# A first chunk in two halves, output stores ahead in SyncE's queue, and half of the attention output transposed by DMA

## The chip, the cores and the metric

The kernel runs on 1 core of one Trainium2 chip. The metric is the device time of one execution in microseconds (us); five runs of the kernel before gave 276.07 to 276.96, median 276.46. The engines are named as in the profile: PE (TensorE matmul) with PEld (its weight loads), DVE (VectorE), ACT (ScalarE), POOL (GpSimd) and SP (SyncE). POOL and SP issue the DMAs; POOL's are those that convert float32 to float16 on the way.

## What is computed

Attention with two kinds of heads, and then a gated feed-forward layer over its output (the reference, cut):

```python
B, H, S, D = 4, 8, 768, 64          # is_retrieval = [1,0,1,0,0,0,1,0]
scores = q @ k.T / sqrt(D)
# heads 0, 2, 6: causal mask; the others: causal, and key < 4 or query - key < 64
a = softmax(where(mask, scores, -1e9));  x = (a @ v)  # tokens x 512, 3072 tokens
g = x @ w_gate;  val = x @ w_val                      # 512 -> 1536 each
ffn = (gelu(g) * val) @ w_out                         # 1536 -> 512
out = x + sigmoid(x @ w_res) * ffn
```

## The kernel before, in words

**Chunks.** The 3072 tokens are six chunks of 512 tokens (four tiles of 128), `CHUNKS` in line 25. A chunk goes through attention, then gate and value, then output. Attention works on four pairs of heads in the order (0,2), (1,3), (4,6), (5,7). For each pair PE computes scores (L783, and L871 for the four sink keys), ACT takes the exponentials (L799, L878), DVE multiplies by masks (L835), PE weighs the values (L900, L910, L924), and DVE divides by the sums (L950 the reciprocals, L961 a float16 copy `x16`, L963 the float32 copy `xtok`; in the even pairs from the second chunk on, the float16 copy is a cast on ACT or DVE, L969/L970). When two pairs are done, four tiles by two column blocks of `x16` are transposed on PE into PSUM (L978, `to_features`, four 128x128 transposes a block) and copied to `xT` by ACT or DVE (L985).

**Gate and value** (`gate_value`, L1003). For each of 12 blocks of 128 hidden columns (f = 0 to 11), PE multiplies `xT` (four column blocks of 128 by 512 tokens) with `wg` and `wv`: 4 + 4 matmuls of 512 columns, those of the column blocks 0 and 1 first and those of 2 and 3 as a second task. ACT takes gelu (L1015), DVE the product (L1017). **Output** (`output`): `res` (L1031), tanh (L1034), 12 matmuls with `wo` a tile (`ff`, L1046), two DVE steps (L1050, L1053), and the store, issued by SP (L1056).

**Loads.** POOL issues, in this order at the start: q and k of the first chunk in four DMAs, four value tiles, `wg` and `wv` in three column parts each (part j serves f = 4j to 4j+3), q and k of the second chunk, `wr`, `wo` in four parts, then value tiles of the second and third chunk. For the first two chunks q and k are transposed on PE (L646); from the third chunk on they are transposed by SP's DMAs (L684, `dT`, 128x512 each, 128 KB in float16). A copy of the values that is shifted by 64 keys (`vs`) is made by two DVE copies in the first chunk (L594) and by SP's DMAs later (L608).

**The order of the work.** A planner in the kernel (`Graph.schedule`) places every task on its engine's queue when the program is built. It holds a price for each task, takes among the ready tasks the one with the lowest priority number, and for a DMA adds an issue time, a transfer time, 0.8 and 1.6 us, and an extra `late` (L289 to L294). `HINTS` (L42) overrides the priorities of single tasks by their number. An engine then works its queue strictly in that order: a task whose input is late holds all tasks behind it. Two rules stand at the end of `build_kernel`: a chunk's scores come after the gate and value of f = 10 of the chunk before (L1090), and its exponentials after that chunk's last gelu (L1092). PE's idle time at the start is filled with matmuls on zeros (L1062, "warm"), which end with the task `g0`.

**PSUM.** Eight banks are shared by kinds (L479): the first chunk's weighted values use `av0`, three slots of two banks; gate and value use `gv`.

Of the kernel before, what the change touches and what calls it, by code (L numbers as in the profile page):

```python
# [6 lines left out]
DHEAD = 64  # L7
# [29 lines left out]
ROWS_UNTIL = 2  # L37

# [4 lines left out]
    "3:-21.19 5:-58.49 6:-58.34 403:490.65 425:595.32 427:528.41 578:-99.99 586:59.9 611:1499.22 612:516.59 "  # L43
    "622:576.96 635:549.35 636:510.21 637:1538.66 643:580.14 647:570.57 648:558.53 649:1085.71 650:1520.19 "
    "653:525.88 654:576.91 655:1026.63 659:511.56 665:514.73 666:516.61 668:1537.73 671:15.77 673:62.65 "
    "677:0.03 679:80.17 680:-75.91 683:82.91 684:-86.3 685:102.37 686:529.24 689:511.01 701:88.3 702:-1.38 "
    "703:114.98 707:516.6 719:1104.93 722:2562.67 733:1538.65 734:1503.99 756:501.37 777:2386.85 816:2334.5 "
    "855:2510.01 861:1434.93 874:2134.02 886:2457.99 922:3352.32 923:1980.91 924:1487.38 972:2502.01 "
    "996:3513.25 1004:2538.32 1026:1534.33 1040:3534.81 1067:2441.52 1090:4509.27 1095:4498.99 1113:4499.01 "
    "1136:4429.99 1139:3502.04 1181:4467.35 1251:4123.82 1253:4130.53 1262:4510.02 1322:5341.74 1368:4505.02 "  # L50
    "1370:5425.02 1394:5537.53 1399:5528.12 1411:5499.01 1412:4524.63 1418:5505.02 1423:5573.53 1424:5090.24 "
    "1444:5424.01 1446:4529.17 1457:5122.53 1458:6525.69 1468:5116.43 1482:4952.05 1485:6442.5 1510:5505.99 "
    "1553:5511.01 1554:5505.99 1608:7485.06 1628:7447.37 1653:7483.11 "
# [391 lines left out]
def build_kernel(nc, q, k, v, w_gate, w_val, w_out, w_res, out):  # L445
# [34 lines left out]
        "av1": (2, one(0, 1)), "av2": (1, [(0, 1)]), "av0": (3, [(0, 1), (6, 7), (2, 3)]),  # L480
        "sc": (2, [(2, 3), (4, 5)]), "scr": (3, one(5, 4, 3, 2)), "scr0": (3, one(6, 5, 4, 3, 2)),
        "gv": (4, one(6, 7, 5, 4, 3, 2)), "gv0": (4, one(6, 7, 5, 4)), "gv00": (2, one(6, 7)), "out": (2, one(6, 7)), "warm": (1, one(7, 5, 1)),
# [56 lines left out]
    def load_weights():  # L539
        for j in range(3):  # L540
            for nm, t, src in (("g", wg, w_gate), ("v", wv, w_val)):
                s = slice(j * 512, (j + 1) * 512)
                wtok[nm, j] = dma("pool", -20 + j, 2.6, (lambda t=t, s=s: lambda: t[:, :, s])(),
                                  src[:, s].rearrange("(ci p) f -> p ci f", p=128))
        wtok["r"] = dma("pool", -12, 2.6, lambda: wr[:, :, :], w_res.rearrange("(ci p) f -> p ci f", p=128))
        for j in range(4):
            s = slice(j * 3, (j + 1) * 3)
            wtok["o", j] = dma("pool", -11 + j, 1.95, (lambda s=s: lambda: wo[:, s, :])(),
                               w_out[j * 384:(j + 1) * 384, :].rearrange("(fi p) c -> p fi c", p=128))

# [14 lines left out]
    def values(b, a, z, base, each, on_engines=False):  # L565
# [21 lines left out]
        if on_engines:  # L587
            ts = []
            for dst, src, off in ((0, 64, 1), (64, 0, 0)):
                def vs(on, dst=dst, src=src, off=off):  # L590
                    def fn(e):
                        o = at(BB.vs)[dst:dst + 64, a_ - 1:z - 1, :, :].rearrange("p i h d -> p (i h d)")
                        i_ = at(BB.v)[src:src + 64, a_ - off:z - off, :, :].rearrange("p i h d -> p (i h d)")
                        return e.activation(out=o, in_=i_, func=AF.Copy) if on == "act" else e.tensor_copy(out=o, in_=i_)  # L594
                    return fn
                n_ = (z - a_) * 520
                ts.append(G.flex({"dve": (c_dve(n_, 3.0, False), vs("dve")), "act": (c_act(n_), vs("act"))},
                                 [BB.vtok[i - off] for i in range(a_, z)], 130, bufs=[BB.v, BB.vs], name="vs"))
            for i in range(a_, z):
                BB.vstok[i] = ts  # L600
            late_copies.extend(ts)
            return
# [13 lines left out]
    def loads_rows(c, si, b, a, z):  # L616
# [18 lines left out]
        values(b, a, z, base + (10 if c == 0 else 8), False, c == 0)  # L635

        per = 1 if c == 0 or n == 4 else 2
        for k_ in range(0, NPAIR, per):
            ps_ = ORDER[k_:k_ + per]
            pr = 1000 * c - 492 + ps_[0] if c else 40 * k_ - 5  # L640
# [29 lines left out]
    def loads_natural(c, si, b, a, z):  # L670
# [5 lines left out]
        for i in range(a, z):  # L676
            for j, src in ((1, k), (0, q)):
# [6 lines left out]
                t = G.add("sp", 1.3, (lambda sv=sv, i=i, j=j: lambda e: e.dma_start(  # L684
# [11 lines left out]
    def attention(c, segs, xbuf, xtbuf, xtoks, xttoks):  # L696
        tiles = [(b, i) for (b, a, z) in segs for i in range(a, z)]
        todo = []
        for k_, p in enumerate(ORDER):
            P = B()  # L700
            P.heads, P.p, P.c, P.pr = PAIRS[p], p, c, 1000 * c + 40 * k_
# [23 lines left out]
        sinks = sink_scores(c, [t for t in tiles if t[1] > 0], 1000 * c + 40 + 5)  # L725
        for t in ph(c, "sc")[:-1]:
            if t.name[2:] in (str(ORDER[2]), str(ORDER[3])):
                t.order.append(ph(c, "sc")[-1])
# [9 lines left out]
        last, norms = None, []  # L738
        for P in todo:
# [3 lines left out]
            last, tn = weigh(P, tiles, sinks, xbuf, x16, xtoks, xdeps, last)  # L743
            if P.heads[0] % 2 == 1:
                for cb in (P.heads[0] // 2, P.heads[1] // 2):
                    to_features(c, cb, P.pr, x16, xdeps, xtbuf, xttoks)
                if P is todo[-1]:
                    tn.order += [t for _, t in xttoks[-2:]]
                if c == 0 and P is todo[-1]:
                    for t in norms[1:]:  # L750
                        t.order.append(xdeps[-1])
            norms.append(tn)

# [87 lines left out]
    def sink_scores(c, need, pr):  # L841

        S = B()
        S.where, S.four, S.et = {}, {}, Buf(P_ek)
        scr = Buf(P_ps, "sc")
        for m, (b, i) in enumerate(need):
            for h in (1, 3, 5, 7):
                S.where[h, b, i] = m * 128
            S.where[4, b, i] = 512
# [3 lines left out]
        cols = (need + need[-1:])[0:4]  # L853
# [13 lines left out]
        for j, (b, i) in enumerate(cols):  # L867
            mms.append((j, batch(b), slice(0, 64), 1, 512, i * 128, 128))

        def sc(e):  # L870
# [7 lines left out]
        S.txs = [G.add("act", c_act(640), lambda e: e.activation(  # L878
            out=at(S.et)[:, 0:640], in_=at(scr)[:, 0:640], func=AF.Exp, scale=SM_SCALE),
            [ts], pr, bufs=[scr, S.et], fset="exp", name="expk")]  # L880
# [3 lines left out]
    def weigh(P, tiles, sinks, xbuf, x16, xtoks, xdeps, last):  # L884
        n = len(tiles)
        c, pr, heads = P.c, P.pr, P.heads
        av = Buf(P_ps, "av2" if c else "av0")
# [3 lines left out]
        def windows(xs, lts):  # L891
            def fn(e):
                r = []
                for x in xs:
                    for lt in lts:
                        b, i = tiles[lt]
                        o, w, BB, h = x * 512 + lt * 65, P.where[x, None, b, i], batch(b), heads[x]
                        for s in range(2):
# [3 lines left out]
                                              start=lt == 0, stop=(i == 0), skip_group_check=True))  # L902
# [3 lines left out]
        def keys(x, lt):  # L906
            def fn(e):
                b, i = tiles[lt]
                o = x * 512 + lt * 65
                return [e.matmul(at(av)[:, o:o + 65], lhsT=at(P.et)[:, P.where[x, kt, b, i]:P.where[x, kt, b, i] + 128],  # L910
                                 rhs=at(batch(b).v)[:, kt, heads[x], :], start=lt == 0 and kt == 0, stop=(kt == i),
# [3 lines left out]
        def sinkf(x, h):  # L915
            def fn(e):
                r = []
                for lt, (b, i) in enumerate(tiles):
                    if i == 0:
                        continue  # L920
                    o, ko = x * 512 + lt * 65, sinks.where[h, b, i]
# [25 lines left out]
        def avv(d0, d1):  # L947
            return at(av).rearrange("p (x w) -> p x w", x=2)[:, :, 0:n * 65].rearrange(
# [8 lines left out]
        xview = lambda: at(xbuf)[:, 0:n, :].rearrange("p i (y x d) -> p x i y d", x=2, d=128)[:, :, :, heads[0] // 4, half]  # L957
        direct = c == 0 or heads[0] % 2
        if direct:

            xdeps.append(G.add("dve", c_dve(2 * n * 64), lambda e: e.tensor_tensor(  # L961
                out=at(x16)[:, :, :, half], in0=avv(0, DHEAD), in1=scale(), op=ALU.mult), [t1], pr - 2.5, bufs=[av, rc, x16], name="norm16"))
        t2 = G.add("dve", c_dve(2 * n * 64), lambda e: e.tensor_tensor(  # L963
            out=xview(), in0=avv(0, DHEAD), in1=scale(), op=ALU.mult), [t1] + xdeps, pr - 2 + (200 if c == 0 and heads[0] else 0), bufs=[av, rc, xbuf], name="norm")
        for i in range(n):
            xtoks.setdefault(i, []).append(t2)
        if not direct:
            def cast(on):
                return lambda e: (e.activation(out=at(x16)[:, :, :, half], in_=xview(), func=AF.Copy) if on == "act" else  # L969
                                  e.tensor_copy(out=at(x16)[:, :, :, half], in_=xview()))  # L970
# [4 lines left out]
    def to_features(c, cb, pr, x16, xdeps, xtbuf, xttoks):  # L975
        n = 4
# [5 lines left out]
        def ev(on):  # L982
            def fn(e):
                o, i_ = at(xtbuf)[:, cb, 0:n * 128], at16(scr)[:, 0:n * 128]
# [7 lines left out]
    def gate_value(c, xtbuf, xttoks):  # L992
# [4 lines left out]
        for f in range(NF):  # L997
            pr = 1000 * c + 500 + f
            kind = "gv" if f > 1 else "gv0" if c or f else "gv00"
# [20 lines left out]
            toks.append(th)  # L1020
# [3 lines left out]
    def output(c, h, htoks, xbuf, xtoks, xtbuf, xttoks):  # L1024
        segs = [(b, t) for (b, a, z) in CHUNKS[c] for t in range(a, z)]
        for lt in range(4):
# [14 lines left out]
            for w in ((slice(0, 256), slice(256, 512)) if last else (slice(0, 512),)):  # L1041
                fb = Buf(P_ps, "gv" if last else "out")
                n = w.stop - w.start
                for j in range(6):
# [3 lines left out]
                        [prev_t, wtok["o", j * 2 // 3], wtok["o", (2 * j + 1) // 3]] + htoks[2 * j:2 * j + 2], pr,  # L1048
# [6 lines left out]
                    [t1] + xtoks[lt], pr + (0 if c == len(CHUNKS) - 1 else 90), bufs=[ot, xbuf], name="add")  # L1055
                G.add("sp", 0.6, (lambda ot=ot, r0=r0, w=w: lambda e: e.dma_start(out[r0:r0 + 128, w], at(ot)[:, w]))(),  # L1056
                      [t2], pr, bufs=[ot], dma=0.75, name="out")
# [13 lines left out]
    firsts = None  # L1071
    for t in late_copies:
        t.order += [x for d in (batches[0].ktok, batches[0].qtok) for (p, i), x in d.items() if i == 0]
    for c, segs in enumerate(CHUNKS):
        xbuf, xtbuf, xtoks, xttoks = Buf(P_x), Buf(P_xt), {}, []
        attention(c, segs, xbuf, xtbuf, xtoks, xttoks)
        firsts = firsts or xttoks
        h, htoks = gate_value(c, xtbuf, xttoks)
# [3 lines left out]
    for c in range(len(CHUNKS)):  # L1082
        gv, gelu = ph(c, "gv"), ph(c, "gelu")
        for f, t in gv:
            t.order += ph(c, "sc") + (ph(c, "xT") if f > (1 if c else 0) else [])
        for t in ph(c, "table"):
            t.order += ph(c, "exp") + ([x for _, x in firsts[:2]] if c == 0 else [])
# [65 lines left out]
```

The softmax here doesn't subtract the row's maximum and nothing guards it: scores larger than these inputs give would overflow.

## Time and profile before

| | |
|---|---|
| median of five runs | 276.46 us (276.07 to 276.96) |
| the profiled execution, its own time | 277.89 us |
| its span, first to last instruction | 276.2 us |
| PE, DVE, ACT, POOL busy | 97%, 51%, 51%, 31% of the span |
| granted TensorE clock, mean | 0.999 |
| first gate matmul (L1003) starts | 23.96 us |
| last `ff` matmul (L1046) ends | 273.04 us |

A row of the timeline gives start and duration in us, engine, line, operation, what it writes and reads, the shapes, how many instructions were merged, and in brackets how long the engine was idle before it and what ended that. Matmuls overlap in the array, so the duration of one (379 ns for 512 columns) is longer than the step from one to the next (216 ns). A "tile" view of a DMA gives, besides the time that its issue takes, the time from issue to landing.

### The profile page before, as it was taken

The page shows a single profiled execution, that of the slowest core. Times are in us where ns is not written, and L with a number is a line of the kernel's source. Part 1 is how long each engine was busy: PE and PEld are TensorE (multiplying, and loading weights), DVE is VectorE, ACT ScalarE, POOL GpSimd, SP SyncE. Part 2 cuts the span into 40 slices and gives each one's busy share as a digit, 9 for nine tenths or more (in the row PEclk, how much of TensorE's full clock was granted, in tenths as well). Part 3 has the DMA queues.
Part 4 walks back from the last instruction along what each step waited for, and adds up shares of the span by engine and source line. Part 5 has one row for each costly group of instructions (what it writes and reads, how often), then busy time and mean ns, then how long its engine had stood idle before and what let it go on. Part 6 is the DMA issues. An engine that isn't in the chain of part 4 may idle for free.

```text
span 276.2 us, 5645 instructions
## 1 busy us (share of the span) xinstructions
PE 268.0 (97%) x2398; PEld 139.5 (51%) x2398; DVE 139.7 (51%) x254; ACT 140.7 (51%) x205; POOL 85.8 (31%) x120
## 2 busy tenths in 40 slices
PE   8987999999899999999999999999999999999995
PEld 8764454455444455544455444455544456544443
DVE  2775263367533367443457533458525256743334
ACT  3745255867324877335675333677333778333410
POOL 8999229991573441992000000000000000000000
PEclk9999999999999999999999999999999999999999
DMA  7999999999999999999911010110100011200022
GB/s 88 169 204 207 185 208 174 150 198 149 136 171 134 237 151 198 136 158 148 191 41 40 0 39 0 40 71 27 60 0 0 1 40 40 78 0 0 0 76 80
DMA packets 92474, 27.81 MB, mean 101 GB/s; under 512 B 81184, under 2 KB 88864, under 8 KB 92448
## 3 DMA queue, kind: packets, MB, share of 16 engines
q0 software_dynamic: 70320, 14.69, 69.4%
q1 hardware_dynamic: 22128, 12.76, 24.2%
q8 instruction: 19, 0.31, 0.5%
q14 instruction: 7, 0.06, 0.1%
HBM read 29.36 MB, written 6.29 MB: 129 GB/s over the span
## 4 chain that ended last, share of the span: by engine, by line
PE 89%; DMA 4%; POOL 3%; DVE 1%; issue 1%; ACT 0%; POOLq 0%
PE ps L1003 44%; PE ps L1046 23%; PE ps L1031 8%; PE ps L783 5%; DMA wg<-in_moe_w_gate_dram 4%; PE ps L910 3%; PE ps L900 2%; PE ps L978 2%; PE ps L924 1%; POOL qks L535 1%; POOL va L535 1%; PE ps L646 1%; DVE hT L1017 1%; PE ps L871 1%; POOL m_win L495 1%
## 5 line engine op out<-in xcount | busy, mean ns | idle before, releaser
L1017 DVE SCALAR_TENSOR_TENSOR hT<-gact,ps 128x512 f16<-128x512 f16 x72 | 48.6, 686 | 73.7 <-ACT gact L1015 48.2
L1003 PE MATMUL ps<-xT,wg 128*128 128x512 f16 x288 | 78.5, 379 | 1.6 <-DMA wg<-in_moe_w_gate_dram 1.1
L1015 ACT ACTIVATE gact<-ps 128x512 f16<-128x512 f32 x72 | 42.8, 597 | 73.0 <-PE ps L1003 67.0
L1003 PE MATMUL ps<-xT,wv 128*128 128x512 f16 x288 | 78.8, 379 | 0.0
L1046 PE MATMUL ps<-wo,hT 128*128 128x512 f16 (+1 forms) x300 | 70.4, 371 | 0.0
L1003 PEld LDWEIGHTS ps<-xT,wg 128*128 128x128 f16 x288 | 27.8, 98 | 34.7 <-DMA wg<-in_moe_w_gate_dram 1.3
L1003 PEld LDWEIGHTS ps<-xT,wv 128*128 128x128 f16 x288 | 27.9, 98 | 33.3 <-DVE hT L1017 0.4
L1046 PEld LDWEIGHTS ps<-wo,hT 128*128 128x128 f16 x300 | 27.0, 98 | 27.5 <-issue 1.5
L799 ACT ACTIVATE er<-ps 128x1024 f16<-128x1024 f32 (+3 forms) x40 | 34.8, 903 | 9.9 <-PE ps L783 9.8
L535 POOL DMA_DIRECT2D qks<-in_k_dram x36 | 28.4, 832 | 32.7 <-DMA qkt<-qks 22.3
L535 POOL DMA_DIRECT2D qks<-in_q_dram x36 | 28.9, 852 | 0.8 <-POOLq L1135 0.8
L1050 DVE SCALAR_TENSOR_TENSOR otile<-srs,ps 128x512 f32<-128x512 f32 (+1 forms) x25 | 16.5, 661 | 24.2 <-PE ps L1046 24.1
L1031 PE MATMUL ps<-wr,xT 128*128 128x512 f16 x96 | 24.6, 380 | 0.0
L535 POOL DMA_DIRECT2D va<-in_v_dram x24 | 21.3, 942 | 6.6 <-PE ps L924 6.6
L1034 ACT ACTIVATE srs<-ps 128x512 f32<-128x512 f32 x24 | 14.3, 597 | 12.3 <-PE ps L1031 12.1
L783 PE MATMUL ps<-qkt 64*128 64x64 f16 (+4 forms) x396 | 17.2, 215 | 0.1
L1053 DVE TENSOR_TENSOR otile<-otile,xtok 128x512 f32<-128x512 f32 (+1 forms) x25 | 16.6, 664 | 0.6
L963 DVE TENSOR_TENSOR xtok<-ps,rcp 128x512 f32<-128x512 f32 x24 | 16.4, 686 | 0.5
L985 ACT ACTIVATE xT<-ps 128x512 f16<-128x512 f16 x12 | 6.8, 596 | 16.0 <-PE ps L978 16.0
L783 PEld LDWEIGHTS ps<-qkt 64*128 64x128 f16 x396 | 10.3, 94 | 7.8 <-issue 3.2
L1062 PE MATMUL ps<-blank 128*128 128x128 f16 x142 | 12.5, 247 | 1.5 <-DVE blank L509 1.1
L1031 PEld LDWEIGHTS ps<-wr,xT 128*128 128x128 f16 x96 | 8.4, 98 | 9.9 <-issue 0.7
(59 smaller groups left out, 197.0 us busy)
## 6 DMA issues: line engine op xcount, KB each, us to landing
out_dram<-otile SPq DMA_DIRECT2D x23, 256.0 KB, 2.4
va<-in_v_dram POOLq DMA_DIRECT2D x24, 128.0 KB, 18.1
qks<-in_k_dram POOLq DMA_DIRECT2D x32, 64.0 KB, 13.7
qks<-in_q_dram POOLq DMA_DIRECT2D x32, 64.0 KB, 13.4
wg<-in_moe_w_gate_dram POOLq DMA_DIRECT2D x3, 512.0 KB, 12.2
wv<-in_moe_w_val_dram POOLq DMA_DIRECT2D x3, 512.0 KB, 14.0
wo<-in_moe_w_out_dram POOLq DMA_DIRECT2D x4, 384.0 KB, 24.6
vs<-va SPq DMA_DIRECT2D x4, 260.0 KB, 5.8
```

The costliest lines, as they stand in the source:

```text
L535: return G.add(eng, issue, lambda e: e.dma_start(out_ap(), in_ap), deps, prio, bufs=bufs, dma=cost, name=name, grp=grp)
L783: return [e.matmul(at(scr)[:, oo:oo + w], lhsT=at(BB.qkt)[half, 1, p, k0:k0 + 128], rhs=at(BB.qkt)[half, 0, p, qq:qq + w], start=True, sto ...
L799: return e.activation(out=o, in_=i_, func=AF.Exp, scale=SM_SCALE)
L963: t2 = G.add("dve", c_dve(2 * n * 64), lambda e: e.tensor_tensor(out=xview(), in0=avv(0, DHEAD), in1=scale(), op=ALU.mult), [t1] + xdeps, ...
L1003: return lambda e: [e.matmul(at(dst)[:, :], lhsT=w[:, ci, f * 128:(f + 1) * 128], rhs=at(xtbuf)[:, ci, :], start=(ci == 0), stop=(ci == NC ...
L1015: ta = G.add("act", c_act(512), (lambda gb=gb, ga=ga: lambda e: e.activation(out=at(ga)[:, :], in_=at(gb)[:, :], func=AF.Gelu))(), [tg], p ...
L1017: th = G.add("dve", c_dve(512), (lambda vb=vb, ga=ga, f=f: lambda e: e.scalar_tensor_tensor(out=at(h)[:, f, :], in0=at(ga)[:, :], scalar=0 ...
L1031: e.matmul(at(rb)[:, :], lhsT=at(xtbuf)[:, ci, s], rhs=wr[:, ci, :], start=(ci == 0), stop=(ci == NCB - 1))
L1034: ta = G.add("act", c_act(512), (lambda rb=rb, sr=sr: lambda e: e.activation(out=at(sr)[:, :], in_=at(rb)[:, :], func=AF.Tanh, scale=0.5)) ...
L1046: e.matmul(at(fb)[:, w], lhsT=at(h)[:, fi, s], rhs=wo[:, fi, w], start=(fi == 0), stop=(fi == NF - 1))
L1050: t1 = G.add("dve", c_dve(n), (lambda fb=fb, sr=sr, ot=ot, w=w: lambda e: e.scalar_tensor_tensor(out=at(ot)[:, w], in0=at(sr)[:, w], scala ...
L1053: t2 = G.add("dve", c_dve(n), (lambda ot=ot, lt=lt, w=w: lambda e: e.tensor_tensor(out=at(ot)[:, w], in0=at(ot)[:, w], in1=at(xbuf)[:, lt, ...
```

## The change

Three parts, and new `HINTS` (92 entries become 126; they give the priorities of single tasks).

**The first chunk in two halves.** Attention of the first chunk is run twice, for tiles 0 and 1 and for tiles 2 and 3; the first half's priorities are 200 lower. Every step has half the width and comes twice. The shifted values are copied for tile 1 alone and for tiles 2 and 3. Gate and value of f = 0 to 3 are then made in halves of 256 tokens; f = 4 to 11 stay whole. The gelu table load no longer waits for two transposed blocks.

**Stores ahead in SP's queue.** The store's priority goes from `1000c + 2400` to 3000 less. The planner's prices for SP's transposes (1.3 to 1.65) and for the landing of stores and of `wo` (`late`) are raised, and the second chunk's value tiles are requested before `wr` and `wo` instead of after them.

**Heads 0 to 3 by DMA.** From the third chunk on (`DT_FIRST = 2`), when the pairs (0,2) and (1,3) are done, one DMA on SP transposes their eight 128x128 blocks (256 KB) from `x16` into `xT`, in place of eight PE transposes and two copies. Heads 4 to 7 stay on PE.

```diff
+DT_FIRST = 2
+DT_ALL = 9
...
-        "av1": (2, one(0, 1)), "av2": (1, [(0, 1)]), "av0": (3, [(0, 1), (6, 7), (2, 3)]),
-        "sc": (2, [(2, 3), (4, 5)]), "scr": (3, one(5, 4, 3, 2)), "scr0": (3, one(6, 5, 4, 3, 2)),
+        "av1": (2, one(0, 1)), "av2": (1, [(0, 1)]), "av1": (3, one(0, 1, 6)),
+        "sc": (2, [(2, 3), (4, 5)]), "scr": (3, one(5, 4, 3, 2)), "scr0": (3, one(5, 4, 3, 2)),
...
+            wtok["o", j].late = 2.2
...
-                ts.append(G.flex({"dve": (c_dve(n_, 3.0, False), vs("dve")), "act": (c_act(n_), vs("act"))},
-                                 [BB.vtok[i - off] for i in range(a_, z)], 130, bufs=[BB.v, BB.vs], name="vs"))
+            for lo, hi, pr in ((1, 2, -75), (2, 4, 130)):
...
+                    ts.append(G.flex({"dve": (c_dve(n_, 2.4, False), vs("dve")), "act": (c_act(n_), vs("act"))},
+                                     [BB.vtok[i - off] for i in range(lo, hi)], pr, bufs=[BB.v, BB.vs], name="vs"))
...
-        values(b, a, z, base + (10 if c == 0 else 8), False, c == 0)
+        values(b, a, z, base + (10 if c == 0 else 2), False, c == 0)
...
-                t = G.add("sp", 1.3, (lambda sv=sv, i=i, j=j: lambda e: e.dma_start(
+                t = G.add("sp", 1.65, (lambda sv=sv, i=i, j=j: lambda e: e.dma_start(
...
-                for cb in (P.heads[0] // 2, P.heads[1] // 2):
-                    to_features(c, cb, P.pr, x16, xdeps, xtbuf, xttoks)
+                if (P.heads[0] < 4 and c >= DT_FIRST) or c >= DT_ALL:
+                    to_features_dma(c, P.heads[0] // 2, P.pr, x16, xdeps, xtbuf, xttoks)
+                else:
+                  for cb in (P.heads[0] // 2, P.heads[1] // 2):
+                    to_features(c, cb, P.pr, x16, xdeps, xtbuf, xttoks, l0, len(tiles))
...
+    def to_features_dma(c, cb, pr, x16, xdeps, xtbuf, xttoks):
+        t = G.add("sp", 1.3, lambda e: e.dma_start(
+            at(xtbuf)[:, cb:cb + 2, :].rearrange("p c (i k) -> p (c i) k", k=128), at(x16)[:, :, :, :].rearrange("p c i k -> p (c i k)"), transpose=True),
+            xdeps, pr - 3, bufs=[x16, xtbuf], dma=1.2, name="xD")
+        t.late = 4.0
+        ph(c, "xT").append(t)
+        xttoks += [(cb, t), (cb + 1, t)]
...
+            if f < len(halves) * 2:
+
+                ths = []
+                for hf, deps in enumerate(halves):
+                    s = slice(256 * hf, 256 * hf + 256)
+                    gb, vb, ga = Buf(P_ps, "gvh"), Buf(P_ps, "gvh"), Buf(P_ga)
...
                 G.add("sp", 0.6, (lambda ot=ot, r0=r0, w=w: lambda e: e.dma_start(out[r0:r0 + 128, w], at(ot)[:, w]))(),
-                      [t2], pr, bufs=[ot], dma=0.75, name="out")
+                      [t2], pr - 3000, bufs=[ot], dma=0.75, name="out").late = 3.0
...
+        if c == 0:
+            last, ek = None, Buf(P_ek)
+            for l0 in (0, 2):
+                halves.append([])
+                last = attention(c, [(0, l0, l0 + 2)], xbuf, xtbuf, xtoks, halves[-1], l0, last, ek)
+                xttoks.extend(halves[-1])
+        else:
+            attention(c, segs, xbuf, xtbuf, xtoks, xttoks)
+        h, htoks = gate_value(c, xtbuf, xttoks, halves)
...
         for t in ph(c, "table"):
-            t.order += ph(c, "exp") + ([x for _, x in firsts[:2]] if c == 0 else [])
+            t.order += ph(c, "exp")
```

## Prediction

> **What bounds the kernel now.** I read the page first: PE is busy 97% of the span, every other compute engine about half. Then the page's slices, to see where PE is not full and how long the DMA engines are:
>
> ```profile
> PE   8987999999899999999999999999999999999995
> ...
> DMA  7999999999999999999911010110100011200022
> ```
>
> A slice is 6.9 us. PE falls below 9 in the first four slices and in the eleventh. The DMA engines are full until about 138 us and nearly idle afterwards. The table by stretches (length, then busy time and count of PE, PEld, DVE, ACT, POOL) says how much PE time is free at all:
>
> ```profile
> 24.00:60.00 36.00, 35.87 (x307) 17.54 (x308) 14.43 (x22) 19.32 (x27) 25.64 (x35) 1.00 1.93 182
> ...
> 69.70:71.70 2.00, 0.85 (x11) 0.47 (x9) 1.18 (x4) 0.60 (x1) 2.00 (x3) 1.00 1.31 95
> 71.70:120.00 48.30, 48.30 (x391) 23.53 (x392) 22.96 (x43) 26.84 (x39) 25.98 (x35) 1.00 1.84 170
> ...
> 200.00:273.00 73.00, 73.00 (x517) 35.69 (x515) 33.70 (x56) 32.48 (x48) 0.00 (x0) 1.00 0.06 23
> ```
>
> From 24 us to 273 us PE stands still for about 1.2 us near 70 us and hardly elsewhere. So there are three places to gain: PE work taken away after 24 us, the hole at 70 us, and work brought forward across 24 us. What holds the start is in the chain of waits (start, length, what):
>
> ```profile
> 11.76 12.15 DMA wg<-in_moe_w_gate_dram
> 23.91 0.05 issue
> 23.96 13.99 PE ps L1003 x64
> ```
>
> The gate waits for the `wg` part issued at 11.76, which is the second part (f = 4 to 7). The tile views of the first parts show that these land earlier:
>
> ```profile
> L535 POOL DMA_DIRECT2D wg<-in_moe_w_gate_dram x1: 772/772/772, 10.0 to 10.0; - x1
> ...
> DMA to landing us min/median/max: 7.8/7.8/7.8
> ```
> ```profile
> L535 POOL DMA_DIRECT2D wv<-in_moe_w_val_dram x1: 780/780/780, 11.0 to 11.0; - x1
> ...
> DMA to landing us min/median/max: 10.4/10.4/10.4
> ```
>
> So `wg` for f = 0 to 3 is there at 17.8 us and `wv` at 21.4. They are unused, since `xT` of all four tiles comes only at 23.45, as DVE's timeline shows:
>
> ```profile
> 14.43 1.60 DVE L594 COPY vs<-va 64x1560 f16<-64x1560 f16 x2 [0.40 <-DMA va<-in_v_dram]
> ...
> 16.40 0.20 DVE L950 RECIPROCAL rcp<-ps 128x8 f32<-128x8 f32 x1
> ...
> 22.69 0.76 DVE L985 COPY xT<-ps 128x512 f16<-128x512 f16 x2
> ```
>
> **The first chunk in halves.** The loads up to `wv` keep their order, so 17.8 and 21.4 stay. First half: its values (tiles 0, 1) land two tile loads earlier, by the step of about 1 us between the value loads, so its shifted copies can run near 14 us and are a third as long. Then DVE has four pairs with a reciprocal (0.20) and a float16 product. That product takes 0.69 at 512 columns; a 256-column DVE step of the output takes 0.42. 4 x 0.62 = 2.5 us. Four `xT` copies at 0.3 (estimate from 0.42 at 512 columns), partly on ACT, are up to 1.2 us; the float32 copies, if not put off, 1.7 us. From a first reciprocal at about 15 us the first half is ready at 18.7 to 20.4. From then PE has the first halves of f = 0 to 3: 4 x 8 matmuls of 256 columns. The step at 512 columns is 216 ns (64 in 13.99 us); half is 0.109, so 3.5 us, of which the value part waits for 21.4. That work ends at about 23 to 24.5.
>
> The second half is later than 23.45: eight DVE products cost 2 x 0.42 instead of 0.69 (+1.2 us), four more reciprocals +0.8, masks and copies some 0.5. Of the before's row about 0.7 us is a float32 copy ahead of `xT` that can be put off. I take 25.5 us (24 to 27.4). Without the halves, PE would have those 3.5 us still ahead of it at 23.96. So the gain is 23.96 + 3.5 - 25.5 = 2.0 us; the ends are 3.5 (second half ready in time) and 0 (at 27.4). Later weights don't bind: f = 4 to 7 begin near 29 us, after `wv` part 2 (26.5), and f = 8 to 11 near 36, after 31.5. Twice as many matmuls in f = 0 to 3 cost nothing if a 256-column step is 0.109; 19 of the last chunk's in a 2.00 us stretch allow 0.12, or +0.7 us for 64. I take +0.1.
>
> **Value tiles ahead of `wr` and `wo`.** Four value loads, about 1.0 us apart, push `wr` from 39.9 to 44 us and the four `wo` parts from 41.8-47.5 to 45.9-51.6. Before, the first `ff` starts at 49.7, after all of `wo`. With 2 us gained it wants to start near 47.7. Cover: `wo` is used part by part, and the second chunk's attention (about 7 us of PE work, whose values now land some 10 us earlier) can fill. Without that cover it costs up to 3 us. I take +0.5. The same earlier values may close the hole at 70 us, where PE waits for the last pair of that chunk: 0 to -1.2, taken as -0.6.
>
> **Transposes by DMA.** Four chunks lose eight transposes each. The view of L978 by stretches:
>
> ```profile
> 106.47:106.92 0.45, 0.44 (x8) 0.27 (x5) 1.00 0.25 28
> ...
> 238.45:238.90 0.45, 0.45 (x8) 0.27 (x5) 1.00 0.24 87
> ```
>
> Eight take 0.45 us and PE is full around them, so 4 x 0.45 = -1.8 us (up to -2.0 with the step to the next matmul). Eight copies of 0.42 to 0.60 on DVE and ACT also go; both are half idle, so nothing.
>
> The Trainium skill, "TensorE: Matmul & The Clock Gate", section "Back-to-back issue gap", gives a sustained step of about 81 ns for 128-column matmuls with their weight loads. By it 32 transposes would be 2.6 us; this trace has 56 ns a step, and the row decides.
>
> What comes in is a wait: PE's gate matmuls now need SP's DMA. Nothing in this trace transposes 256 KB; the nearest rows are `dT` (128 KB), in the third chunk's stretch and after it:
>
> ```profile
> L684 SPq DMA_TRANSPOSE qkt<-qks x10: 1188/1210/2107, 106.6 to 122.0; - x10
> ...
> DMA to landing us min/median/max: 4.4/5.0/6.1
> ```
> ```profile
> L684 SPq DMA_TRANSPOSE qkt<-qks x2: 1264/1328/1391, 128.5 to 129.9; - x2
> ...
> DMA to landing us min/median/max: 4.2/4.9/5.5
> ```
>
> One more issue of 1.2 to 1.3 us on top makes 5.4 to 6.8 us when quiet and up to 7.4 in the third chunk, plus up to 2.1 behind a `dT` in SP's queue, which is occupied almost without a break from 106.6 to 123. If all of it doubles, it is 8.4 to 11.0, and 14.3 in the third chunk. Between the first transposes and the long run of gate matmuls there are now 6.9, 7.0, 5.0 and 5.7 us of other PE work in the four chunks. But the planner's price is 1.3 + 0.8 + 1.2 + 1.6 + 4.0 = 8.9 us, so the new order should put that much work between, and there is enough: the output of the chunk before is 64 matmuls, 13.8 us. If it comes late, everything on PE waits behind the gate matmul. Excess over 8.9: 0 from the single-step rows; from the doubled ones up to 5.4 + 3 x 2.1 = 11.7. I take +0.3, near the rows.
>
> The Trainium skill, "DMA: Bandwidth & Descriptors", section "Latency and other measured facts", gives 261 GB/s for a transposing DMA. By it 256 KB would move in 1.0 us and the second half would add 0.5, not 1.2 to 1.3; the distance would be kept with more to spare.
>
> **Stores ahead.** Three stores of the first chunk now wait for 16 `dT` (until 87.5 us), and nobody on DVE or PE waits for them, so moving them saves nothing. Ahead of the `dT` they delay these by about 0.5 us each; the third chunk's `dT` land by 77 us and its scores start near 90. Cost 0. Late chunks have an idle SP.
>
> **Sum.** -2.0 + 0.1 + 0.5 - 0.6 - 1.8 + 0.3 = -3.5 us. The profiled execution took 277.89 (span 276.2), which becomes 274.4 (272.7). The median of the runs is 1.4 below it: 276.46 - 3.5 = 273.0.
>
> **Rivals.**
> A: the first chunk gives nothing. Either the second half is ready only at 27.4 us (DVE is 87% busy from 10 to 20 us and gets more instructions), or PE, in strict order, stands at a value matmul until 21.4 with the second half's attention behind it, or 2 us are lost again at `wo`. Against it: 3.5 us of first-half work have their weights. 276.46 - 1.8 - 0.6 + 0.9 = 275.0.
> B: slower. The 256 KB transposes land later than the planner's 8.9 us, in each of four chunks. They decide once the sum of lateness is over 3.8 us, about 1 us a chunk, a landing near 9.9 us after `x16`. At 10.5 us: 276.46 - 3.8 + 4 x 1.6 = 279.1. For it: `dT` with all queues full had a median of 8.0 (56 to 80 us). Against it: three of the four chunks have idle DMA engines.
> C: the parts cancel: no gain at the start and the 1.8 us of transposes go into waiting: 276.4.
>
> **Chances.** Forecast 0.58, A 0.21, C 0.05, B 0.16. Faster by over 0.2% (0.55 us, about what a measurement can tell) 0.79, within it 0.05, slower 0.16. The range takes in the full gains, 276.46 - 3.5 - 2.0 - 1.2 = 269.8, and at the top A, C and the beginning of B: 277.3.
>
> **What would show it.** First L1003 near 20 us, with 256 columns and the first `wg` part; 256-column work until about 24, then a gap under 2 us. No idle PE between 40 and 55 us. 64 transposes of `to_features` on PE in place of 96. SP's new transposes landing 5.5 to 8.5 us after issue, and no wait of L1003 for a DMA on `xT`. Wrong would be: such waits of over 1 us in each of the last four chunks, the first gate still at 23.9, or PE waiting for `wo`.

## The result, and the profile after

The changed kernel takes 275.59 us (median of 45 runs, 274.20 to 278.89), the kernel before beside it 276.50 (85 runs). The ratio is 0.9964, with a 95% interval of 0.9953 to 0.9974: faster by 0.9 us, where 3.5 was forecast. The profiled execution took 275.73 us with a span of 273.7. That is 2.2 us under the profiled execution of before (277.89), so more than half of what the two traces show apart is not there between the medians.

The page's slices after, in the same two rows as shown for before:

```profile
PE   6999999999999999899999999999999999999995
...
DMA  6999999999999999999932200014100013200013
```

The eleventh slice (the hole near 70 us) is full now, and the seventeenth (about 109 to 116 us) has a dent that was not there. In the DMA row the late part, which had bumps of up to 2 tenths before, has some of up to 4; three of the new transposes stand there, at 142, 184 and 227 us. The table by stretches (length, then busy time and count of PE, PEld, DVE, ACT, POOL, the granted clock, DMA share, GB/s) says the same in microseconds:

```profile
24.00:60.00 36.00, 35.45 (x344) 19.89 (x342) 17.82 (x37) 21.01 (x34) 23.05 (x31) 1.00 1.74 187
60.00:75.00 15.00, 15.00 (x137) 7.87 (x136) 9.77 (x17) 7.27 (x13) 10.91 (x14) 1.00 1.61 177
...
113.00:200.00 87.00, 87.00 (x701) 41.77 (x699) 45.18 (x79) 42.31 (x62) 9.02 (x12) 1.00 0.61 82
```

PE's timeline at the start (start, duration, engine, line, operation, shapes, count, and in brackets the idle time before):

```profile
20.69 0.60 PE L1034 MATMUL ps<-xT,wv 128*128 128x256 f16 x4
...
25.72 0.59 PE L1052 MATMUL ps<-xT,wv 128*128 128x512 f16 x2
...
27.73 0.60 PE L1052 MATMUL ps<-xT,wg 128*128 128x512 f16 x2 [0.55 <-DMA wg<-in_moe_w_gate_dram]
```

Gate and value begin at 20.69 us in halves (L1034). At 25.72 come the first matmuls over all 512 tokens (L1052), so by then the second half's column blocks 0 and 1 are ready. At 27.73 PE waits for the third part of `wg`. The chain of waits around the dent (start, length, what):

```profile
102.46 0.26 PE ps L1095 x2
102.72 8.38 DMA xT<-x
...
111.14 1.90 PE ps L1052 x8
```

The chain of waits leaves PE and runs for 8.38 us through one transfer, the third chunk's transposing DMA; PE stood idle for 1.30 us of that.

### The profile page after: what moved, and what is told of

It is laid out like the page before. It is cut to its first block, busy times and chain, and to the rows that moved or that the text cites. A ratio compares the mean times of both kernels' runs of the same rounds, so it can differ in the third digit from the quotient of the medians.

```text
span 273.7 us, 5654 instructions
## 1 busy us (share of the span) xinstructions
PE 266.1 (97%) x2381; PEld 138.8 (51%) x2381; DVE 142.0 (52%) x277; ACT 138.8 (51%) x212; POOL 85.8 (31%) x120
## 4 chain that ended last, share of the span: by engine, by line
PE 86%; DMA 8%; POOL 4%; issue 1%; DVE 0%; POOLq 0%
PE ps L1052 43%; PE ps L1095 22%; PE ps L1080 7%; DMA wg<-in_moe_w_gate_dram 5%; PE ps L798 5%; DMA xT<-x 3%; PE ps L931 3%; PE ps L921 2%; PE ps L1034 1%; PE ps L945 1%; POOL qks L541 1%; POOL va L541 1%; PE ps L1006 1%; PE ps L654 1%; PE ps L889 1%
## 5 line engine op out<-in xcount | busy, mean ns | idle before, releaser
L1066 DVE SCALAR_TENSOR_TENSOR hT<-gact,ps 128x512 f16<-128x512 f16 x68 | 46.2, 687 | 70.4 <-ACT gact L1064 42.9
L1064 ACT ACTIVATE gact<-ps 128x512 f16<-128x512 f32 x68 | 40.4, 597 | 74.4 <-PE ps L1052 68.7
L1052 PE MATMUL ps<-xT,wg 128*128 128x512 f16 x272 | 75.1, 379 | 1.9 <-DMA xT<-x 1.3
L1052 PE MATMUL ps<-xT,wv 128*128 128x512 f16 x272 | 76.1, 379 | 0.0
L1095 PE MATMUL ps<-wo,hT 128*128 128x512 f16 (+1 forms) x300 | 69.5, 371 | 0.0
L1052 PEld LDWEIGHTS ps<-xT,wg 128*128 128x128 f16 x272 | 26.4, 98 | 34.1 <-DMA xT<-x 1.8
L1052 PEld LDWEIGHTS ps<-xT,wv 128*128 128x128 f16 x272 | 25.8, 98 | 30.4 <-DVE otile L1099 1.0
L814 ACT ACTIVATE er<-ps 128x1024 f16<-128x1024 f32 (+4 forms) x40 | 34.1, 891 | 10.5 <-PE ps L798 10.2
L1083 ACT ACTIVATE srs<-ps 128x512 f32<-128x512 f32 x24 | 14.3, 596 | 11.4 <-PE ps L1080 11.2
L984 DVE TENSOR_TENSOR xtok<-ps,rcp 128x512 f32<-128x512 f32 (+1 forms) x28 | 16.9, 607 | 0.4
L814 ACT ACTIVATE es<-ps 128x1024 f16<-128x1024 f32 (+1 forms) x14 | 12.6, 900 | 4.4 <-PE ps L798 4.4
## 6 DMA issues: line engine op xcount, KB each, us to landing
wg<-in_moe_w_gate_dram POOLq DMA_DIRECT2D x3, 512.0 KB, 10.3
```

The source lines that it names most:

```text
L814: return e.activation(out=o, in_=i_, func=AF.Exp, scale=SM_SCALE)
L1052: return lambda e: [e.matmul(at(dst)[:, :], lhsT=w[:, ci, f * 128:(f + 1) * 128], rhs=at(xtbuf)[:, ci, :], start=(ci == 0), stop=(ci == NC ...
L1064: ta = G.add("act", c_act(512), (lambda gb=gb, ga=ga: lambda e: e.activation(out=at(ga)[:, :], in_=at(gb)[:, :], func=AF.Gelu))(), [tg], p ...
L1066: th = G.add("dve", c_dve(512), (lambda vb=vb, ga=ga, f=f: lambda e: e.scalar_tensor_tensor(out=at(h)[:, f, :], in0=at(ga)[:, :], scalar=0 ...
L1083: ta = G.add("act", c_act(512), (lambda rb=rb, sr=sr: lambda e: e.activation(out=at(sr)[:, :], in_=at(rb)[:, :], func=AF.Tanh, scale=0.5)) ...
L1095: e.matmul(at(fb)[:, w], lhsT=at(h)[:, fi, s], rhs=wo[:, fi, w], start=(fi == 0), stop=(fi == NF - 1))
```

## The experiments

Where the order of the tasks had to be worked out anew, the kernel's own planner did that. Line numbers in the rows are those of each kernel.

**Both kernels again: how far is one execution from another?** Two more profiled executions of the kernel before and one of the changed kernel, no edit.

> The kernel before, unchanged, profiled again. The profiled execution of before took 277.89 us, 1.4 us over the median. Theory S (its start was late by chance): here the second wg part lands near 22 us instead of 23.91 and the first gate matmul starts at 22.4 to 23.0, with the span 1 to 1.5 us shorter. Rival (the profiled start is the usual one): wg part 2 lands at 23.7 to 24.1 again and the first gate matmul at 23.9.

> The same once more, to see how far the landing of the weights and the hole near 70 us move from execution to execution. Theory S: first gate matmul between 22.3 and 24, not always 23.96. Rival: 23.9 each time.

> The kernel after, unchanged, profiled again. If the wait for the transposing DMA in the third chunk is systematic, PE stands still again for 1 to 2 us near 110 us before the first gate matmul of that chunk, and in no later chunk. If it was chance, the wait is gone here. The wait for the third wg part (0.55 us at 27.7) is expected to vary between 0 and 1 us.

276.23, 276.92 and 275.29 us. The chain of waits at the start, of the first of them:

```profile
11.78 10.47 DMA wg<-in_moe_w_gate_dram
...
22.30 3.84 PE ps L1003 x17
```

and of the second:

```profile
11.76 11.19 DMA wg<-in_moe_w_gate_dram
...
22.99 3.20 PE ps L1003 x14
```

The same DMA, issued at the same time, took 12.15 us in the execution that the prediction was made from. From the first gate matmul to the end of the span it is 252.2 us in all three (276.2 - 23.96, 274.5 - 22.30, 275.2 - 22.99). So what differs between executions of the kernel before is when `wg`'s second part lands, and the prediction's execution had it 1 to 1.7 us late. The hole near 70 us (0.69 and 0.47 us idle, the same in all three) and, in the changed kernel, the wait in the third chunk (1.05 us here, 1.30 before) came again. The changed kernel's start moves too: here its second half was ready at 26.51 us, 0.8 later than in the other execution.

**The transposing DMAs from the fourth chunk on.** The changed kernel with one number changed. The eight transposes that come back shift the task numbers that `HINTS` names, so these are mapped: all other tasks keep their priorities.

```diff
-DT_FIRST = 2
+DT_FIRST = 3
```

> The kernel after, with DT_FIRST = 3: the third chunk's heads 0 to 3 are transposed on PE again, the other three chunks by DMA. Theory W (the third chunk's DMA costs more than it saves): 0.45 us of transposes come back, a wait of 1.25 us goes, so 0.8 us faster than after, 274.8 us. Rival (the wait only shows idle time that would stand elsewhere): same as after or 0.45 us slower, 275.6 to 276.0.

274.41 us, ratio 0.9915 (0.9897 to 0.9932). PE has no idle time over 0.2 us from its first gate matmul to the end. The view of the three DMAs left:

```profile
L1002 SPq DMA_TRANSPOSE xT<-x x3: 1237/1247/1787, 141.4 to 225.9; - x3
...
DMA to landing us min/median/max: 3.0/3.1/3.1
```

A transfer of 256 KB lands 3.1 us after its issue in these chunks. The same view of the changed kernel, for the third chunk alone:

```profile
L997 SPq DMA_TRANSPOSE xT<-x x1: 1597/1597/1597, 102.7 to 102.7; - x1
...
  PE ps L1052: 1.3, 1
...
DMA to landing us min/median/max: 8.4/8.4/8.4
```

The table by stretches of the changed kernel, while the third and the fourth chunk's transfer were under way (the DMA share is the last but one):

```profile
102.72:111.10 8.38, 7.12 (x76) 3.78 (x74) 6.30 (x13) 4.02 (x6) 8.25 (x12) 1.00 1.82 171
142.26:145.31 3.05, 3.05 (x48) 1.70 (x47) 2.56 (x6) 1.05 (x2) 0.00 (x0) 1.00 0.45 86
```

It is the place in the program that makes the wait: with a DMA share of 1.82 the transfer takes 8.4 us, with 0.45 it takes 3.05, and taking this one DMA away brings 1.2 us.

**The first chunk whole.** The changed kernel, with attention and gate of the first chunk as in the kernel before, and the order worked out anew.

```diff
-            for l0 in (0, 2):
-                halves.append([])
-                last = attention(c, [(0, l0, l0 + 2)], xbuf, xtbuf, xtoks, halves[-1], l0, last, ek)
-                xttoks.extend(halves[-1])
+        attention(c, segs, xbuf, xtbuf, xtoks, xttoks)
...
-        h, htoks = gate_value(c, xtbuf, xttoks, halves)
+        h, htoks = gate_value(c, xtbuf, xttoks)
```

> The kernel after with the first chunk whole, as before (attention once over four tiles, no halves in gate and value, the first chunk's priorities of before; the later ones are after's, adapted). Theory H (the halves gain nothing, since before usually starts its gate at 22.3 to 23.0 and after has only 4 of 192 gate and value matmuls done then): equal to after or 0.8 us faster, 274.8 to 275.6. Rival (the halves gain the 2 us that were forecast): 277.5 us.

274.70 us, ratio 0.9926 (0.9899 to 0.9954). The first reading was that the halves cost 0.9 us. But in the new order the third chunk's DMA also just met its matmul: it was issued at 104.68, landed 5.7 us later (the DMA share was 1.40 in that time), and the matmul started at 110.42. So the wait of 1.3 us had gone with the halves. The run doesn't separate the two; the four kernels at the end do.

**Every transpose on PE.** The changed kernel without its DMAs, the order from the third chunk on worked out anew.

```diff
-DT_FIRST = 2
+DT_FIRST = 9
```

> The kernel after with all transposes of the attention output on PE (DT_FIRST = 9; priorities from the third chunk on adapted to it). Theory W: 4 x 0.45 us come back and the wait of 1.25 us near 110 us goes: 0.5 us slower than after, 276.1 us. Rival (the DMA transposes of the last three chunks gain nothing either): 274.4 us, as fast as with the DMA from the fourth chunk on.

275.19 us, ratio 0.9931 (0.9906 to 0.9956), where the changed kernel has 0.9964 (0.9953 to 0.9974). Together the four DMAs of the change gain nothing; if anything they lose some 0.4 us.

**The earlier value tiles alone.** The kernel before, with the same priorities, and the two edits that put the second chunk's values ahead of `wr` and `wo`.

```diff
+            wtok["o", j].late = 2.2
...
-        values(b, a, z, base + (10 if c == 0 else 8), False, c == 0)
+        values(b, a, z, base + (10 if c == 0 else 2), False, c == 0)
```

> The kernel before with one part of the change: the second chunk's value tiles are requested ahead of wr and wo, and the planner's price for the landing of wo is 2.2 us higher. Theory V (the earlier values close the hole of about 1.5 us near 70 us and the later wo costs nothing): 275.0 to 275.3 us, no idle PE near 70 us and none between 45 and 55 us. Rival (the hole is the planner's order, not the values): still there, 276.5 us or slower by a wait for wo of up to 2 us.

286.75 us, ratio 1.0359 (1.0323 to 1.0395): 10 us slower. The hole near 70 us is gone, and one of 9.4 us, which ends at 92.9, has come. Three views of this kernel, read backwards. PE's timeline:

```profile
92.91 1.89 PE L1006 MATMUL ps<-xT,wg 128*128 128x512 f16 x4 [9.41 <-DVE otile L1053]
```

DVE's timeline:

```profile
92.17 0.69 DVE L1053 SCALAR_TENSOR_TENSOR otile<-srs,ps 128x512 f32<-128x512 f32 x1 [10.46 <-DMA out_dram<-otile]
```

SP's queue:

```profile
56.46 14.15 SPq L687 DMA_TRANSPOSE qkt<-qks  x8
70.65 0.61 SPq L611 DMA_DIRECT2D vs<-va  x1
71.36 14.07 SPq L687 DMA_TRANSPOSE qkt<-qks  x8
85.47 1.63 SPq L1059 DMA_DIRECT2D out_dram<-otile  x3
```

PE waits for VectorE, VectorE for one of three output buffers, and the stores of all three stand behind 16 transposes in SP's queue, until 85.47 us. With the values there earlier, the planner had moved the second chunk's attention forward and the first chunk's fourth output tile behind it, to a time when all three buffers are taken. In the kernel before that never happens: in the first of its repeats the first store leaves at 52.4 us, so that the fourth tile can come at 64.6, and the fifth comes at 95.4, after the stores that left at 86.6.

**The same, with three stores ahead.** Only SP's queue differs from the run just told; every engine's own order is kept. For the first chunk's first three stores:

```diff
+    for t, n in zip(moved, (0, 2, 5)):
+        queue.insert(queue.index(turned[n]), t)
```

(`turned` are the 16 transposes.) Beside it the kernel before with its own stores 2 to 4 moved in the same way and nothing else (`(2, 5, 8)`).

> The kernel with the value tiles ahead of the weights (286.75 us), with the first chunk's first three stores moved ahead in SyncE's queue: in front of the first, the third and the sixth of its 16 transposing DMAs instead of behind all of them. Every engine's own order stays as it was. Theory S (the stores ahead are what makes the earlier value tiles usable: the 10.46 us that VectorE waited at 92 us for a free output tile end with them, and the clock that fell after it stays up): the hole at 92.9 us and the one at 70 us are both gone, and the whole is 1.0 to 1.5 us under the kernel before, 275.0 to 275.7. Theory 0 of the prediction (nobody waits for the stores): 286.7 again.

> The kernel before with only SyncE's queue changed: the first chunk's stores 2 to 4 go in front of the third, sixth and ninth of the 16 transposing DMAs. In the kernel before only VectorE's fifth output tile, at 95 us, needs one of these buffers again, and the stores left at 86.6 us. Theory S: no effect by itself, 276.5 within 0.3 (0.2 us worse if the transposes that stand 0.6 us later each are missed at 70 us). Rival: the stores by themselves are worth something, 275.5 or less.

With the values: 275.52 us, ratio 0.9969 (0.9954 to 0.9984). Without them: 276.40 us, ratio 1.0002 (0.9987 to 1.0017). SP's queue in the first of the two:

```profile
54.87 0.90 SPq L1075 DMA_DIRECT2D out_dram<-otile  x1
55.81 2.79 SPq L703 DMA_TRANSPOSE qkt<-qks  x2
59.39 0.36 SPq L1075 DMA_DIRECT2D out_dram<-otile  x1
59.80 4.88 SPq L703 DMA_TRANSPOSE qkt<-qks  x3
64.72 0.58 SPq L1075 DMA_DIRECT2D out_dram<-otile  x1
```

The stores leave at 55 to 65 us, the wait on VectorE is gone, and the hole near 70 us (1.16 us idle) stays closed. A new gap of 0.43 us stands at 49.33, where PE waits for an exponential of ACT. So the stores are worth nothing by themselves, the values alone cost 10 us, and both together gain 0.9 us. This pair has none of the halves and no transposing DMA, and has as much gain as the whole change.

**The stores back behind, in the changed kernel.** The kernel with the DMAs from the fourth chunk on, with its first chunk's stores 2 to 4 put behind the 16 transposes.

```diff
+    held = [t for t in queue if t.name == "out"][1:4]
+    queue = [t for t in queue if t not in held]
+    after = queue.index([t for t in queue if t.name == "dT"][15]) + 1
+    G.prog["sp"] = queue[:after] + held + queue[after:]
```

> The kernel with the DMA transposes from the fourth chunk on, its order unchanged on every engine but SP: the first chunk's second to fourth store are put behind the 16 transposes of the third and fourth chunk, about where before had them. Theory 0 (nobody waits for these stores): as fast, 274.4 us. Rival (the output tiles come free too late and PE waits through DVE): 1 to 3 us slower, with a wait of the DVE step of the output near 85 to 95 us.

278.97 us, ratio 1.0071 (1.0044 to 1.0097), against 274.41 with the stores ahead. PE's and DVE's timelines show the same wait:

```profile
96.75 0.60 PE L1116 MATMUL ps<-wo,hT 128*128 128x512 f16 x2 [3.35 <-DVE otile L1120]
```
```profile
96.00 0.69 DVE L1120 SCALAR_TENSOR_TENSOR otile<-srs,ps 128x512 f32<-128x512 f32 x1 [5.65 <-DMA out_dram<-otile]
```

The hole of 3.35 us is most of the 4.6. This profiled execution is the fastest of nine (277.49); what the others took longer is told in the last section.

**What are the halves worth? Four kernels on one chip.** First chunk whole or in halves, crossed with every transpose on PE or heads 0 to 3 by DMA from the fourth chunk on; values and stores are ahead in all four. Three of them are kernels already told (the values with the stores; every transpose on PE; DMAs from the fourth chunk). The fourth, whole with DMAs from the fourth chunk and its order worked out anew, had been run once before:

> The changed kernel with the first chunk whole and the transposing DMAs from the fourth chunk on, its later order worked out anew: the two edits that cost in the runs before are both taken out. If the two gains add (0.9 from the whole first chunk, 1.2 from the fourth chunk), 273.5; if the order of the work swallows the one of them, as the whole chunk's run already had no wait in the third chunk, 274.2 to 274.6.

That gave 274.27 us, ratio 0.9913 (0.9894 to 0.9932). All four, side by side:

> First of four kernels on the same chip: first chunk whole or in halves, and every transpose on PE or heads 0 to 3 by DMA from the fourth chunk on. All four have the value tiles and the stores ahead. This one: whole, PE (the kernel before with the value tiles and stores moved). Expected 275.5, as before.

> Whole, DMA from the fourth chunk on. If the three chunks' 24 transposes of 0.45 us for eight are all gained, it is 1.35 us under the first of the four: 274.2. If most of it is lost in waiting, 275.2.

> Halves, PE. Theory N (the halves are worth nothing: the gate starts 1.4 us earlier but gives the time back to the first chunk's attention that is still owed): within 0.3 of the first, 275.2 to 275.8. Rival H+ (the halves gain 1 us, as the ratio of the earlier runs on different chips would have it): 274.5. Rival H- (they cost 0.9): 276.4.

> Halves, DMA from the fourth chunk on. Theory N: within 0.3 of the second of the four. Rival H+: 1 us under it. Rival H-: 0.9 over it. For the DMAs it says the same as the second against the first: 1.35 us under the third if the transposes are all gained.

| | first chunk whole | in halves |
|---|---|---|
| transposes on PE | 275.68, ratio 0.9980 (0.9959 to 1.0002) | 275.02, ratio 0.9948 (0.9933 to 0.9962) |
| heads 0 to 3 by DMA from the fourth chunk | 273.83, ratio 0.9907 (0.9893 to 0.9921) | 274.57, ratio 0.9939 (0.9919 to 0.9959) |

Read across, the halves gain 0.7 us in the one row and lose 0.7 in the other: no gain that holds in both orders, and the intervals exclude 2.0 us in both. Read down, the DMAs gain 1.85 and 0.45 us; the intervals of the second pair overlap, so its 0.45 is not told from nothing. PE's groups by shape give what they take off PE. In the kernel with halves and all transposes on PE, and then with the DMAs:

```profile
L1023 PE MATMUL ps<-ident,x 128*128 128x128 f16 x96 | 7.9, 219 | 0.0
```
```profile
L1011 PE MATMUL ps<-ident,x 128*128 128x128 f16 x72 | 6.1, 219 | 0.0
```

24 transposes fewer. Their steps from one matmul to the next add up to 5.55 us with PE alone and 4.12 with the DMAs: 1.4 us less, close to the 1.35 of the prediction's row (3 x 0.45) and between the two measured gains. A part of the difference can be read. The whole kernel with all transposes on PE has the gap near 50 us:

```profile
50.17 0.50 PE L802 MATMUL ps<-qkt 64*128 64x256 f16 x8 [0.43 <-ACT es L818]
```

None of the other three is idle for over 0.2 us after its first gate matmul. So 0.43 us of the 1.85, and of the 0.7 that the halves gain in that row, go with this gap. The rest is not settled; each of the four has its own order.

The halves can be followed on PE. In the kernel with halves and DMAs:

```profile
21.46 0.60 PE L1039 MATMUL ps<-xT,wv 128*128 128x256 f16 x4
...
26.50 0.59 PE L1057 MATMUL ps<-xT,wv 128*128 128x512 f16 x2
```

and with the whole chunk and DMAs:

```profile
22.48 2.33 PE L1041 MATMUL ps<-xT,wg 128*128 128x512 f16 x10 [0.55 <-DMA wg<-in_moe_w_gate_dram]
```

Between 21.46 and 26.50 the halves do 32 matmuls of 256 columns, worth 16 of 512, and attention of the second half in between. The whole chunk starts 1.0 us later but has nothing between: (26.50 - 22.48) / 0.216 = 18.6. It is 0.6 us ahead. In the other whole kernel of the four `wg`'s second part landed later, the first gate was at 23.41, and the same sum gives 14.3: 0.4 us behind. So the halves start earlier, without `wg`'s second part, but PE spends that lead on the second half's attention, which the whole chunk has behind it when it waits for the weights. What is left is a few tenths to either side, by when that part lands.

## Why the prediction was wrong

**The start, forecast -2.0, measured about 0.** This is the failed step, and the largest. The views of the first half were nearly right: first gate at 20.69 (18.7 to 20.4 forecast), second half ready at 25.72 (25.5). What failed is the 23.96 in "23.96 + 3.5 - 25.5", and the line "The median of the runs is 1.4 below it: 276.46 - 3.5 = 273.0" with it. The 1.4 us by which that execution lay above the median was the late landing of `wg`'s second part, which is also what the halves were to gain. The gain was counted against an execution with the loss in it, and then taken off a median without it. With the 22.30 of another execution: 22.30 + 3.5 - 25.7 = 0.1; the two repeats of before and the two executions of the changed kernel give -0.7 to +0.8 (22.30 + 3.5 - 26.51; 22.99 + 3.5 - 25.72). The four kernels agree, within their 0.7 to either side. "Later weights don't bind" was wrong by a little: at 27.73 PE waited 0.55 us for `wg`'s third part in the one execution, and not in the other. Rival A, no gain at the start, came nearest with 275.0, but by luck: none of its three reasons came. Rival C (276.4) had the right two parts, no gain at the start and the transposes' gain gone into waiting, and missed the hole at 70 us that closed.

**The third chunk's DMA, forecast +0.3, measured +1.05 to +1.3.** The term was mis-sized: PE's wait was 1.30 and 1.05 us in the two executions, and the runs with and without this DMA are 1.2 apart, net of the eight PE transposes that it saves. The doubled rows ("8.4 to 11.0") were the ones that came. SP's queue in the changed kernel:

```profile
100.94 0.58 SPq L1106 DMA_DIRECT2D out_dram<-otile  x1
101.57 1.10 SPq L616 DMA_DIRECT2D vs<-va  x2
102.72 1.60 SPq L997 DMA_TRANSPOSE xT<-x  x1
```

`x16` was complete at 100.33 us (its last product runs on DVE from 99.65 for 0.68). The end of a run of transposes (to 100.90), a store and two copies of the values stood before the DMA, 2.4 us together, then it took 8.4 us: 10.8 in all, against the planner's 8.9. Rival B named the mechanism and its point (about 9.9 us), but for all four chunks. In the last three it lands in 3.0 to 3.8 us, even less than the 5.4 to 6.8 forecast. One reason is that the forecast added the second half as a second issue: 256 KB take 1.25 us to issue here, where 128 KB took 1.2 to 1.3 as well. The other is that the row that it took as quiet was not: in the kernel before the DMA share was 2.01 from 128.50 to 135.40, while these two `dT` were under way, against 0.38 to 0.46 under the last three transfers. The Trainium skill, "DMA: Bandwidth & Descriptors", section "Latency and other measured facts", gives 261 GB/s for a transposing DMA with a non-contiguous middle dimension; the estimate from it, 0.5 us for a second half, pointed the right way for these three chunks, though no run here sets that half apart, and the third chunk's 8.4 us shows nothing of that rate.

**The transposes, forecast -1.8.** Right in size as work of PE: 24 of them are 1.4 us of PE steps by the profiles. All 32 gain nothing together, because with the halves the 24 brought only 0.45 us to the end and the third chunk's DMA took 1.2 back.

**The hole at 70 us, forecast -0.6, and `wr` and `wo` later, +0.5.** The hole closed altogether (-1.2, its idle time). `wo`'s parts land at 45.1 to 50.8 us, a little before the forecast 45.9 to 51.6, and PE waited for none of them. Both terms were better than forecast, together by about 1.1 us.

**Stores ahead, "Cost 0", "nobody on DVE or PE waits for them".** True of the kernel before, as the run with the stores alone shows, and wrong for the change. The values and the stores were priced apart; the values make the waiter. Left behind, the stores cost 4.6 us (278.97 against 274.41), of which 3.1 at the full clock (277.49, the profiled execution).

The sum, from runs with the halves: values, stores and halves without any DMA -1.5 (275.02 against 276.55), the three quiet DMAs -0.45 (274.57), the third chunk's DMA +1.2 (275.59 against 274.41). That makes -0.8 where -0.9 was measured. The steps follow one another through the same kernels, so that the sum comes out proves little; it says where the time went. What it leaves open is the middle term: PE's steps show 1.4 us less work there, and in this order of the tasks only a third of it reached the end.

## What to carry to other kernels

When one profiled execution lies above the median, find out which wait makes the difference before pricing an edit to that same wait, or the gain is counted twice: here two more profiles of the unchanged kernel showed it. A store held back by its queue costs nothing until an order of work appears that needs its buffer; so price an edit to the order together with the buffers that it fills, and each of the edits alone as well as together. And price a moved transfer where it will stand, by what moves on the queues at that time: the same DMA took 3.0 us or 8.4.

The fastest of these kernels leaves out what did not pay: first chunk whole, values and stores ahead, DMAs from the fourth chunk on: 273.83 us, ratio 0.9907 (0.9893 to 0.9921), and 274.27 in its earlier run. From the changed kernel it is enough to write `DT_FIRST = 3` and to keep the numbers in `HINTS` on their tasks: 274.41.

## What was not expected of the hardware

After the stall of the run with the values alone, PE came back slow. The table by stretches of that kernel (PE's busy time and count first, the granted clock third from the end):

```profile
93.00:97.00 4.00, 4.00 (x12) 1.44 (x13) 1.78 (x3) 0.60 (x1) 4.00 (x7) 0.58 1.92 202
97.00:101.00 4.00, 4.00 (x26) 1.66 (x25) 2.22 (x6) 2.89 (x5) 0.75 (x2) 1.00 2.18 153
```

From 93 to 97 us the granted clock was 0.58. In shorter stretches of the same trace (PE alone) it leaves 1.00 at about 86.1 us, 2.6 after PE's last matmul, stands at 0.50, and comes back at about 96.35, 3.4 after PE had started again:

```profile
86.00:86.50 0.50, 0.00 (x0) 0.61 1.64 159
...
96.00:96.50 0.50, 0.50 (x3) 0.65 2.39 151
```

From 92.91 to 96.30 PE did 8 matmuls of 512 columns; at the usual step of 0.216 us they take 1.7. So this stall cost about 1.7 us more than it lasted. With the 9.4 of the stall and the new 0.43 near 50 us, less the 1.2 of the closed hole, that makes 10.3 where 10.0 was measured.

After the hole of 3.35 us in the kernel with the stores back behind, the granted clock was 1.00 in the profiled execution:

```profile
97.00:101.00 4.00, 4.00 (x80) 2.36 (x79) 1.78 (x4) 2.70 (x4) 4.00 (x6) 1.00 3.02 183
```

That execution is not the usual one. Of this kernel's nine, two show a mean clock of 1.00 over the span (277.49 and 277.73 us); the other seven show 0.988 to 0.994 and took 278.53 to 280.33, 1.4 us more from median to median. The likely reading is that this hole costs clock in most executions, but no kept trace shows where in the span the clock fell, or how long the hole was there. So these runs give no safe length for a hole: one trace lost the clock after 2.6 us of idleness, another kept it through 3.35.
